# GraphSAGE mean aggregation on one core: 256 buckets' source features fetched by indirect row transfers, and two small kinds of ScalarE work moved to GpSimd

## The chip, the core and the metric

The kernel runs on one core of a Trainium2 chip. The metric is the device time of one execution in microseconds (us). Before the change it is 1871.68 us, the median of three runs (1863.13 to 1876.03).

The engines are named as in the profile: PE is TensorE, DVE VectorE, ACT ScalarE, POOL GpSimd, SP SyncE. SP issues DMAs from its own queue, POOL from another; each engine works through its instructions in the order in which they were written.

## The reference

800,000 edges join 12,500 nodes with 64 features each. For every edge the features of its source node are added to its destination node, the sums are scaled by `deg_inv`, and two 64 x 64 weight matrices are applied:

```python
N, deg, D = 12500, 64, 64
E = N * deg
nsum = _segment_sum(x[src], dst, N)
h_neigh = nsum * deg_inv[:, None]
return x @ w_self + h_neigh @ w_neigh
```

## The kernel before

**Sorting.** Each edge becomes one 32-bit key, made of the destination's block (77 blocks of 164 nodes), the source's block (98 blocks of 128 nodes), the destination's half block, the source's place in its block and the destination's place in its half. The pair of a destination block and a source block is a bucket; there are 77 * 98 = 7546, and a bucket has 128 slots (64 for each half of the destination block). The keys are sorted in 128 runs on DVE (`sort_runs`), cut into rows, gathered with indirect DMAs (`gather_runs` L533, `split_rows` L543) and merged (`merge_runs` L572). The rows come in three parts, with 29, 20 and 10 buckets to a row and 128 rows each: buckets 0 to 3711, 3712 to 6271, and the rest.

**Decoding a part** (L746 to L855). For each of a row's buckets, `find_and_gather` counts the keys below the bucket's first key (DVE, L708), turns the count into a position `ix` with one small ACT instruction (L762), and fetches a window `v` of keys around that position with an indirect DMA on POOL (L742). `decode_buckets` splits the window: the sources' places in their block go as a bfloat16 list `l` to the DRAM table `sl` (L794), one row of 128 slots per bucket, and the destinations' places are transposed by PE into the SBUF table `dlT`. Part 0 is decoded before the last stage begins; parts 1 and 2 are decoded inside it, between the steps described next. Keys that did not fit in a bucket's slots are found apart (`leftovers` L865); there are 127 groups of 128 of them.

**The last stage** (`nodes`, L943). Its loop walks the buckets in tiles of 8. `one_hots` (L924) prepares 28 buckets at a time: SP loads the 28 rows of `sl`, spread over all partitions, into `slb` (four DMAs, L933); DVE compares them with the partition's number and gets the one-hot matrices `ohs`, 128 sources by 128 slots for each bucket (L935); and it compares the destinations' places with a ramp and gets `ohd` (L940). `gather` then lets PE multiply each bucket's `ohs` with the source block's features `xh`, which stay in SBUF (L966; 128 fp16 numbers per node, 64 leading and 64 trailing parts). That puts the features of each slot's source into PSUM, `ct`; ACT copies the 8 buckets to SBUF as `xg` (L976), or DVE does, for some tiles of part 2 (L974). `sums` lets PE multiply `xg` with `ohd`, in two halves, into the accumulators `acc` (L1047). For the leftovers, POOL fetches 128 rows of features from the DRAM table `xt` with one indirect DMA into one of five buffers `lx` (L997), up to 616 buckets ahead, and PE adds them (L1015).

**What sets the order.** All these instructions are written in one order by hand: for each tile the loop writes a `gather`, every other tile two `sums`, in between a step of the part being decoded, and after that DVE merge steps for the next part, until `PACE` nanoseconds of them (420, later 405, by the program's own costs) are written per tile (L1361). So the merges ride along with the tiles, and DVE's queue holds both. SP's queue holds the loads of `slb`, each waiting for one of three buffers. POOL's queue holds the fetches of `lx`, `v` and `u` (the gathers of `split_rows`), and the writing of the outputs.

**Finishing** (L1105). When six destination blocks are done, PE multiplies the sums with the weights into `po`, ACT scales the result with `deg`, one instruction for each 123 nodes, as a copy from PSUM to SBUF (L1117), and in a later step POOL adds it to the output in DRAM (L1123).

Of the kernel before, what the change touches and what calls it, by code (L numbers as in the profile page):

```python
# [23 lines left out]
NB = 98  # L24
# [13 lines left out]
SPARE = TURN - BASE[2]  # L38
assert 128 * KPRS[2] < BASE[1]
# [4 lines left out]
        (32, 48, 72, 124, 204, 368, 676, 1264))  # L44
SUP = 8
# [6 lines left out]
PACE = (0, 420, 405)  # L52
# [20 lines left out]
LAG = 4  # L73
HELD = 5
OCT = 6
# [78 lines left out]
def constants():  # L154
# [15 lines left out]
    assert out["cx"].shape == (128, NCX)  # L170
    for p in range(NP):
# [202 lines left out]
class Kernel:  # L374
# [12 lines left out]
    def setup(self):  # L387
# [23 lines left out]
        self.cx = keep.tile([128, NCX], F32, name="cx")  # L411
        self.junkb = keep.tile([128, JUNKB], BF, name="junkb")
# [53 lines left out]
    def sort_edges(self, mps):  # L466
# [10 lines left out]
        with tc.tile_pool(name="raw", bufs=1) as raw:  # L477
            with tc.manual_schedule():
                self.make_keys(raw, a, mps)
                nc.sync.dma_start(self.c1, self.I["c1"])  # L480
                nc.sync.dma_start(self.cx, self.I["cx"])
                for p in range(NP):
                    nc.sync.dma_start(self.c2[p], self.I[f"c2_{p}"])
# [262 lines left out]
    def find_and_gather(self, part, vp):  # L746
# [8 lines left out]
        for k in range(kpr + LAG):  # L755
# [4 lines left out]
            if k >= LAG:  # L760
                g = k - LAG
                nc.scalar.activation(ix[:, g:g + 1], acc[:, g:g + 1], AF.Relu, bias=self.c2[part][:, 3, g:g + 1])  # L762
# [3 lines left out]
    def decode_buckets(self, part, v, vp, mps):  # L766
# [21 lines left out]
        def narrow(k, n, vk, w):  # L788
# [4 lines left out]
            rows = self.sl[BASE[part]:BASE[part] + 128 * kpr].rearrange("(r k) s -> r k s", k=kpr)  # L793
            (nc.gpsimd if part else nc.sync).dma_start(rows[:, k:k + n], l16[:, :n])  # L794
# [129 lines left out]
    def one_hots(self, pool):  # L924
# [3 lines left out]
        for c in range(0, NBID, 28):  # L928
            n = min(28, NBID - c)
# [4 lines left out]
            s = pool.tile([128, 28, 128], FH, name="ohs", bufs=3)[:, :n]  # L934
            nc.vector.tensor_scalar(s.rearrange("p c s -> p (c s)"), b, self.pidx[:, :1], None, op0=OP.is_equal)  # L935
            d = pool.tile([128, 14, HN, 2], FH, name="ohd", bufs=4)[:, :n // 2]
# [4 lines left out]
            yield [(s[:, j], d[:, j // 2, :, j % 2]) for j in range(n)]  # L941

    def nodes(self, pool, aps, mps):  # L943
# [3 lines left out]
        source = self.one_hots(pool)  # L947
        ready = []
        pend = []
        late = []  # L950
        done = []
        acc = None

        turn = 0

        def gather(b0, cnt, vector):
# [4 lines left out]
            while len(ready) < min(cnt + ahead, NBID - b0):  # L961
                ready.extend(next(source))
            cols = ready[:cnt]
            del ready[:cnt]
            for i in reversed(range(cnt)):
                nc.tensor.matmul(ct[:, i * 128:(i + 1) * 128], cols[i][0],  # L966
                                 self.xh[:, (b0 + i) % NB].rearrange("p a f -> p (a f)"), start=True, stop=True)
            xg = pool.tile([128, 1024], FH, name="xg", bufs=6)
            if vector and (len(ready) < min(8 + ahead, NBID - b0 - cnt) or NBID - b0 < 56):
# [3 lines left out]
            if vector and turn % 2:  # L973
                nc.vector.tensor_copy(xg[:, :cnt * 128], ct[:, :cnt * 128])  # L974
            else:
                nc.scalar.activation(xg[:, :cnt * 128], ct[:, :cnt * 128], AF.Copy)  # L976
            return b0, xg, [d for _, d in cols]
# [11 lines left out]
        def pick(b0):  # L989
            if self.picked == len(done) or len([u for u in uses if u[5]]) >= HELD:  # L990
# [11 lines left out]
        def spread(u):  # L1002
            o, p, c, f, e = u[:5]
            u[7] = pool.tile([128, 2, OCT * HN], FH, name="ohl", bufs=HELD)
            n = slice((f - o * OCT) * HN, (e - o * OCT) * HN)
            nc.vector.tensor_scalar(u[7][:, :, n], self.wide.rearrange("p (h n) -> p h n", h=2)[:, :, n],
# [4 lines left out]
        def add(u, stop=False):  # L1011
            o, _, _, f, e = u[:5]
            n = slice((f - o * OCT) * HN, (e - o * OCT) * HN)
            for h in range(2):
                nc.tensor.matmul(acc[h][:, n], u[5], u[7][:, h, n], start=False, stop=stop)  # L1015
# [11 lines left out]
        def sums(job):  # L1027
# [15 lines left out]
            for i, d in enumerate(cols):  # L1043
# [369 lines left out]
```

## Time and profile before

| | |
|---|---|
| median of three runs | 1871.68 us |
| the profiled execution | 1856.37 us |
| its span, first to last instruction | 1854.6 us |
| busy in the span: DVE, ACT, PE, POOL | 1718.2, 1116.7, 986.6, 576.2 us |
| first and last `ohs` matmul of the last stage (L966) | 804.6 and 1836.7 us |
| bytes read from HBM, written to it | 277.01, 26.52 MB |

The span's first 804.6 us are sorting, merging and decoding part 0, with DVE nearly alone at work; the last stage takes the rest. A group of instructions is shown as line, engine, operation, output<-input and shape, its count, busy time and mean duration in ns, and then the idle time of its engine just before it, with what ended that idle time. A window of the span is shown as from:to, its length, and then each engine's busy time with the number of its instructions in brackets; after that the granted TensorE clock, the share of the 16 DMA engines that was busy, and GB/s.

### The profile page before, as it was taken

The numbers are of one execution on the slowest core, as the hardware profiler recorded it, in microseconds if no ns is written. First come the engines' busy times: TensorE is split into PE (matmuls) and PEld (weight loads), VectorE is DVE, ScalarE is ACT, GpSimd is POOL, SyncE is SP. The second block draws the span as 40 slices with busy tenths as digits, with TensorE's granted clock in tenths as the row PEclk, the third lists the DMA queues.
The fourth block names the chain that finished last, engine by engine and source line by source line (L and its number), as shares of the span: only waits on it lengthen the run. The fifth ranks groups of instructions, "written<-read, shape, count | busy, mean of one in ns | idle before, by whom it ended". The sixth has DMA issues, their size and how long they took to land.

```text
span 1854.6 us, 54153 instructions
## 1 busy us (share of the span) xinstructions
PE 986.6 (53%) x23413; PEld 851.9 (46%) x23413; DVE 1718.2 (93%) x1718; ACT 1116.7 (60%) x1587; POOL 576.2 (31%) x447
## 2 busy tenths in 40 slices
PE   3046000000000000058979979897898899888996
PEld 1015000000000000057868868776887788777885
DVE  6999999999999999989989999998898799978885
ACT  5263000113001005458979989899999899977885
POOL 2000000055502005404456535473332523532331
PEclk7567555555555555579989999999999999999998
DMA  5207100021002002169978888996889788977894
GB/s 174 54 0 169 39 0 0 38 79 51 18 4 73 10 0 82 47 216 266 274 249 253 251 248 254 296 282 227 264 250 284 234 265 242 326 200 257 274 268 118
DMA packets 176789, 307.79 MB, mean 166 GB/s; under 512 B 127885, under 2 KB 133596, under 8 KB 175772
## 3 DMA queue, kind: packets, MB, share of 16 engines
q1 hardware_dynamic: 98268, 275.58, 44.9%
q0 software_dynamic: 78272, 28.65, 9.6%
q8 instruction: 185, 3.03, 0.7%
q14 instruction: 64, 0.52, 0.1%
HBM read 277.01 MB, written 26.52 MB: 164 GB/s over the span
## 4 chain that ended last, share of the span: by engine, by line
DVE 19%; PE 13%; DMA 11%; issue 10%; SPq 5%; POOL 4%; ACT 4%; DVEq 0%; POOLq 0%; ACTq 0%
DMA slb<-sl 10%; PE ct L966 7%; DVE u L328 7%; PE acc L1047 5%; SPq L933 5%; DVE ohs L935 4%; DVE ohd L940 3%; ACT xg L976 2%; DVE u L362 2%; POOL u L565 1%; POOL lx L997 1%; POOL out L1123 1%; DVE u L316 1%; DMA sl<-l 1%; PE acc L1015 1%
## 5 line engine op out<-in xcount | busy, mean ns | idle before, releaser
L976 ACT ACTIVATE xg<-ct 128x1024 f16<-128x1024 f32 x919 | 862.6, 1074 | 104.4 <-PE ct L966 80.0
L966 PE MATMUL ct<-xh,ohs 128*128 128x128 f16 x7546 | 532.6, 224 | 87.9 <-DVE ohs L935 23.7
L966 PEld LDWEIGHTS <-ohs 128*128 128x128 f16 x7546 | 451.8, 100 | 125.4 <-issue 52.5
L328 DVE TENSOR_TENSOR u<-u 128x1512 f32<-128x1512 f32 (+57 forms) x316 | 425.7, 1362 | 12.9 <-ACT u L312 8.6
L1047 PE MATMUL acc<-ohd,xg 64*128 64x82 f16 x15092 | 395.2, 201 | 47.7 <-ACT xg L976 20.4
L1047 PEld LDWEIGHTS <-xg 64*128 64x128 f16 x15092 | 324.6, 96 | 104.6 <-issue 29.2
L997 POOL DMA_INDIRECT lx<-xt,ls x127 | 232.0, 1826 | 425.6 <-PE acc L1015 352.5
L940 DVE TENSOR_TENSOR ohd<-iota,dlT 128x2296 f16<-128x2296 bf16 x270 | 362.2, 1341 | 0.0
L935 DVE TENSOR_SCALAR ohs<-slb,pidx 128x3584 f16<-128x3584 bf16 x270 | 321.8, 1192 | 40.2 <-DMA slb<-sl 19.0
L509 PE MATMUL stp<-cx,swapa 128*128 128x16 f32 (+1 forms) x12 | 3.1, 335 | 398.0 <-DVE swapa L505 398.0
L260 DVE TENSOR_TENSOR a<-b 128x1040 f32<-128x1040 f32 (+41 forms) x130 | 194.7, 1539 | 3.5 <-DVE b L260 0.5
L260 DVE TENSOR_TENSOR b<-a 128x1040 f32<-128x1040 f32 (+46 forms) x150 | 194.6, 1345 | 3.2 <-ACT a L262 0.4
L538 POOL DMA_INDIRECT u<-d,ixa x48 | 72.5, 1511 | 390.8 <-ACT junka L526 335.4
L509 PEld LDWEIGHTS stp<-cx,swapa 128*128 128x128 f32 x12 | 2.6, 271 | 398.5 <-DVE swapa L505 398.5
L312 ACT ACTIVATE u<-u 128x256 f32<-128x256 f32 (+14 forms) x60 | 33.0, 618 | 170.6 <-DVE u L316 134.8
L1123 POOL DMA_DIRECT2D out<-o x27 | 99.1, 3800 | 103.1 <-ACT o L1117 89.8
L802 PE MATMUL tr<-idb,l 128*128 128x128 bf16 x59 | 7.6, 263 | 188.9 <-ACT l L796 188.9
L262 ACT ACTIVATE b<-a 128x2 f32<-128x2 f32 (+31 forms) x41 | 15.9, 402 | 127.1 <-DVE a L260 120.4
L802 PEld LDWEIGHTS <-l 128*128 128x128 bf16 x59 | 4.3, 114 | 191.2 <-ACT l L796 190.8
L316 DVE TENSOR_TENSOR u<-u 128x2016 f32<-128x2016 f32 (+11 forms) x40 | 61.9, 1563 | 16.2 <-DMA u<-da,ixb 8.8
L262 ACT ACTIVATE a<-b 128x1 f32<-128x1 f32 (+24 forms) x34 | 8.6, 259 | 105.4 <-DVE b L260 99.9
L565 POOL DMA_INDIRECT u<-da,ixb x24 | 36.9, 1539 | 88.6 <-ACT ixb L513 85.0
(158 smaller groups left out, 839.4 us busy)
## 6 DMA issues: line engine op xcount, KB each, us to landing
slb<-sl SPq DMA_DIRECT2D x1076, 224.0 KB
xt<-xh SPq DMA_DIRECT2D x1, 3136.0 KB
out<-o POOLq DMA_DIRECT2D x25, 123.0 KB
own<-os SPq DMA_DIRECT2D x12, 256.0 KB
out<-os SPq DMA_DIRECT2D x12, 256.0 KB
rd<-dst SPq DMA_DIRECT2D x5, 512.0 KB
rs<-src SPq DMA_DIRECT2D x5, 512.0 KB
lx<-xt,ls POOLq DMA_INDIRECT x127
```

The lines of the kernel that those rows point to most:

```text
L260: nc.vector.tensor_tensor(view(dst, lo + sh, [[st, g], [1, l]]), x, y, op=op)
L316: nc.vector.tensor_tensor(at(oth, to, n), x, y, op=op)
L328: nc.vector.tensor_tensor(to, at(cur, ln + lo, n), at(cur, lo + k, n), op=op)
L538: nc.gpsimd.indirect_dma_start(out=u[:, i * w:(i + 1) * w], out_offset=None, in_=src, in_offset=bass.IndirectOffsetOnAxis(ap=self.start[pa ...
L933: nc.sync.dma_start(b[j::4], bass.AP(tensor=src.tensor, offset=src.offset, ap=[[0, 32], [1, n * 128]]))
L935: nc.vector.tensor_scalar(s.rearrange("p c s -> p (c s)"), b, self.pidx[:, :1], None, op0=OP.is_equal)
L940: nc.vector.tensor_tensor(d, self.iota[:, None].to_broadcast(wide), ix, op=OP.is_equal)
L966: nc.tensor.matmul(ct[:, i * 128:(i + 1) * 128], cols[i][0], self.xh[:, (b0 + i) % NB].rearrange("p a f -> p (a f)"), start=True, stop=True)
L976: nc.scalar.activation(xg[:, :cnt * 128], ct[:, :cnt * 128], AF.Copy)
L997: nc.gpsimd.indirect_dma_start(out=x, out_offset=None, in_=self.xt, in_offset=bass.IndirectOffsetOnAxis(ap=self.left[p][1][:, c:c + 1].bit ...
L1047: nc.tensor.matmul(acc[h][:, db % OCT * HN:(db % OCT + 1) * HN], xg[r, i * 128:(i + 1) * 128], d[r], start=db % OCT == 0 and sb == 0, stop ...
L1123: nc.gpsimd.dma_start(out, o[:n, at], accum_op=OP.add)
```

## The change

**Direct buckets.** In part 0 the bucket in column 15 of each row, in part 1 the one in column 11, is direct: 128 in each part, one in 29 and one in 20. A direct bucket has no row in `sl`, no `ohs`, no `L966` matmul and no place in `ct` and `xg`. Its list of sources is transposed by PE when its part is decoded (a tile `dt`), and three DVE instructions on 128 x 128 turn it into row numbers of `xt` (`dix`). In the last stage one indirect DMA on POOL per direct bucket fetches its 128 slots' rows from `xt` into one of 12 buffers `xd` (`bring`), at most one per tile, 160 buckets ahead of the tile; the `acc` matmul reads `xd` in place of a piece of `xg`. `ohd` is made as before, now by a generator of its own (`dest_hots`). A tile holds up to 8 buckets that are not direct, and the direct ones between them: there are 914 tiles in place of 950 (449, 305 and 160 by part, before 467, 322 and 161).

**Moved to POOL.** The position `ix` is made by a POOL `tensor_scalar` on 128 x 1 directly ahead of the fetch that reads it. In finishing, ACT copies `po` in one instruction for all 492 nodes, and POOL multiplies it in place with `deg` (123 x 256).

**Beside that**, `PACE` becomes 428 and 430, a leftover buffer is picked only when fewer than five are in use or were added in the last six tiles (`BACK`), and the leftovers' destination matrix `ohl` is stored narrower. The core of the diff:

```diff
+DCOL = (15, 11, None)
+KSRC = [k - (c is not None) for k, c in zip(KPRS, DCOL)]
+DIRECT = {BASE[p] + r * KPRS[p] + c: (p, r) for p, c in enumerate(DCOL) if c is not None for r in range(128)}
+NSRC = NBID - len(DIRECT)
+FETCH = 160
+FETCHED = 12
...
-PACE = (0, 420, 405)
+PACE = (0, 428, 430)
...
+DCH = 28
 HELD = 5
...
+BACK = 6
...
-                nc.scalar.activation(ix[:, g:g + 1], acc[:, g:g + 1], AF.Relu, bias=self.c2[part][:, 3, g:g + 1])
+                nc.gpsimd.tensor_scalar(ix[:, g:g + 1], acc[:, g:g + 1], self.c2[part][:, 3, g:g + 1], None, op0=OP.add)
                 self.gather_window(part, g, ix)
...
+            (nc.gpsimd if part else nc.sync).dma_start(rows[:, to:to + m], l16[:, :m])
+            if m < n:
+                ps = mps.tile([128, 128], BF, name="dt", tag="ct", bufs=3)
+                nc.tensor.transpose(ps, l16[:, m], self.idb)
+                u = vp.tile([128, 128], F32, name="du")
+                nc.vector.tensor_tensor(u, ps, self.dx[:, part], op=OP.add)
+                nc.vector.scalar_tensor_tensor(u, ps, 128.0, u, op0=OP.is_lt, op1=OP.mult)
+                self.direct[part] = self.keep.tile([128, 128], U32, name=f"dix{part}")
+                nc.vector.tensor_scalar(self.direct[part], u, float(N), None, op0=OP.add)
+                self.spent += 800
...
-        for c in range(0, NBID, 28):
-            n = min(28, NBID - c)
+        for c in range(0, NSRC, 28):
+            n = min(28, NSRC - c)
...
+        def bring(b0, most):
+
+            while most and coming and coming[0][0] <= b0 + FETCH and coming[0][1][0] in self.direct:
+                b, (p, r) = coming.pop()
+                coming.extend(islice(fetch, 1))
+                held[b] = pool.tile([128, 128], FH, name="xd", bufs=FETCHED)
+                nc.gpsimd.indirect_dma_start(
+                    out=held[b], out_offset=None, in_=self.xt,
+                    in_offset=bass.IndirectOffsetOnAxis(ap=self.direct[p][:, r:r + 1], axis=0))
+                most -= 1
...
+            own = [b for b in range(b0, b0 + cnt) if b not in DIRECT]
+            num = len(own)
...
+            parts = {b: xg[:, i * 128:(i + 1) * 128] for i, b in enumerate(own)}
+            return b0, [parts[b] if b in parts else held.pop(b) for b in range(b0, b0 + cnt)], dest
...
-            if self.picked == len(done) or len([u for u in uses if u[5]]) >= HELD:
+            busy = len([u for u in uses if u[5]]) + len([n for n in added if n > len(done) - BACK])
+            if self.picked == len(done) or busy >= HELD:
                 return
...
+        tiles = TILES
+        bring(0, 8)
         for t, (b0, cnt) in enumerate(tiles):
+            bring(b0, 1)
             pend.append(gather(b0, cnt, self.changed))
...
-            for b in range(b0, b0 + nb):
-                nc.scalar.activation(o[:n, b], po[:n, b], AF.Copy, scale=self.deg[:n, 4 * qq + b:4 * qq + b + 1])
+            at = slice(b0, b0 + nb)
+            nc.scalar.activation(o[:n, at], po[:n, at], AF.Copy)
+            scale = self.deg[:n, 4 * qq + b0:4 * qq + b0 + nb]
+            nc.gpsimd.tensor_tensor(o[:n, at], o[:n, at], scale[:, :, None].to_broadcast([n, nb, D]), op=OP.mult)
```

In the built program the lines of the changed kernel are other numbers: `xd` is fetched at L1016, `lx` at L1073, the multiplication with `deg` stands at L1196, the output's DMA at L1202, `ix` at L788 and the fetch of `v` at L768. Three places show how the instructions stand.

POOL in part 1, after the gathers of part 2's rows and up to the store of the merged rows. Before:

```order
L997 DMA lx<-xt,ls_16204 128x128 x3
L1123 DMA out<-o 123x4x64
L997 DMA lx<-xt,ls_16204 128x128
L1123 DMA out<-o 123x4x64
L997 DMA lx<-xt,ls_16204 128x128 x7
L1123 DMA out<-o 123x4x64
```

The same place in the changed kernel, as far as the second output (`dix_15020` holds part 1's row numbers):

```order
L1073 DMA lx<-xt,ls_16649 128x128
L1016 DMA xd<-xt,dix_15020 128x128 x3
L1196 TENSOR_TENSOR o<-o,deg 123x256
L1016 DMA xd<-xt,dix_15020 128x128 x2
L1073 DMA lx<-xt,ls_16649 128x128
L1202 DMA out<-o 123x4x64
L1016 DMA xd<-xt,dix_15020 128x128
L1073 DMA lx<-xt,ls_16649 128x128
L1016 DMA xd<-xt,dix_15020 128x128 x4
L1196 TENSOR_TENSOR o<-o,deg 123x256
L1073 DMA lx<-xt,ls_16649 128x128
L1016 DMA xd<-xt,dix_15020 128x128 x2
```

Between two fetches of `lx` now stand up to five of `xd`, and the multiplication stands some fetches ahead of the DMA that writes its result.

POOL where part 2's windows are fetched. Before:

```order
L595 DMA d_2_71<-u 128x1264
L742 DMA v<-d_2_71,ix_2_23618 128x200
L997 DMA lx<-xt,ls_16204 128x128
L742 DMA v<-d_2_71,ix_2_23618 128x200 x5
L997 DMA lx<-xt,ls_16204 128x128
```

In the changed kernel, the first of them:

```order
L621 DMA d_2_71<-u 128x1264
L1016 DMA xd<-xt,dix_15020 128x128 x2
L1073 DMA lx<-xt,ls_16649 128x128
L1016 DMA xd<-xt,dix_15020 128x128
L788 TENSOR_SCALAR ix_2_23846<-acc_2_23845,c_2_74 128x1
L768 DMA v<-d_2_71,ix_2_23846 128x200
L1016 DMA xd<-xt,dix_15020 128x128
L788 TENSOR_SCALAR ix_2_23846<-acc_2_23845,c_2_74 128x1
L768 DMA v<-d_2_71,ix_2_23846 128x200
L1016 DMA xd<-xt,dix_15020 128x128
```

Each fetch of `v` has its `ix` ahead of it on POOL itself, and fetches of `xd` between.

ACT around the finishing of six destination blocks in part 0. Before:

```order
L1054 ACTIVATE g<-acc_6437 128x6x82
L976 ACTIVATE xg<-ct 128x1024 x4
L1117 ACTIVATE o<-po,deg 123x64 x4
L976 ACTIVATE xg<-ct 128x1024 x15
L1117 ACTIVATE o<-po,deg 123x64 x4
```

In the changed kernel:

```order
L1132 ACTIVATE g<-acc_6467 128x6x82
L1050 ACTIVATE xg<-ct 128x1024 x2
L1194 ACTIVATE o<-po 123x256
L1050 ACTIVATE xg<-ct 128x1024 x15
L1194 ACTIVATE o<-po 123x256
```

Four small instructions became one.

More of the change, by code (lines that the diff above doesn't have):

```diff
@@ L951, in nodes @@
         done = []
+        added = []
         acc = None
         turn = 0
+        left = [NSRC, NBID]
+        fetch = iter(sorted(DIRECT.items()))
+        coming = [next(fetch)]
+        held = {}
+        def bring(b0, most):
[7 more added lines that the diff above has]
+                most -= 1
         def gather(b0, cnt, vector):
```

97 lines of the change are left out of this document (64 added, 33 removed).

## The prediction

> **What bounds the kernel now.** I first cut the span by stage (the view of busy time by window), at the first matmul of the last stage and at the points where the new fetches of part 0 and of part 1 end, 160 buckets ahead of the part's last one.
>
> ```profile
> 0.00:804.60 804.60, 75.01 (x274) 43.48 (x274) 762.27 (x575) 186.58 (x400) 153.04 (x206) 0.54 0.18 50
> 804.60:1301.00 496.40, 431.73 (x10837) 380.48 (x10838) 472.11 (x562) 452.78 (x577) 230.29 (x128) 0.96 0.86 262
> 1301.00:1650.00 349.00, 311.79 (x7867) 276.19 (x7867) 318.08 (x399) 326.77 (x433) 140.24 (x85) 0.97 0.85 259
> 1650.00:1854.60 204.60, 168.09 (x4447) 151.76 (x4441) 165.75 (x187) 150.57 (x180) 52.60 (x28) 0.95 0.76 229
> ```
>
> The columns after the length are PE, PEld, DVE, ACT, POOL. Until 804.6 the change has nothing to do. In the next two windows, which I call A and B, no engine alone is the bound: DVE is busy for 95% and 91%, ACT 91% and 94%, PE 87% and 89%, the DMA engines 86% and 85%. Only POOL has room: 46% and 40%. Next the view of waits, for 804.6 to 1650: who holds up PE, the end of the pipeline.
>
> ```profile
> POOL lx L997 <- PE acc L1015: 267.9, 57, 13.2
> POOL out L1123 <- ACT o L1117: 48.0, 11, 13.7
> PE ct L966 <- DVE ohs L935: 23.7, 19, 8.2
> PE ct L966 <- ACT xg L976: 20.8, 22, 3.8
> PE acc L1047 <- ACT xg L976: 20.4, 15, 4.8
> DVE ohs L935 <- DMA slb<-sl: 11.0, 12, 2.3
> ```
>
> PE loses 41 us to ACT and 24 to DVE. POOL's long waits are for a free `lx` buffer: POOL is early, and nobody waits for it.
>
> **What the change takes away.** The groups of instructions from 800 us on give the prices (busy time, mean ns, idle time before):
>
> ```profile
> L976 ACT ACTIVATE xg<-ct 128x1024 f16<-128x1024 f32 x906 | 857.8, 1080 | 103.7 <-PE ct L966 79.3 <-DMA slb<-sl 22.4 <-PE acc L1015 0.7
> L966 PE MATMUL ct<-xh,ohs 128*128 128x128 f16 x7546 | 532.6, 224 | 87.9 <-DVE ohs L935 23.7 <-ACT xg L976 22.3 <-DMA slb<-sl 22.0
> L935 DVE TENSOR_SCALAR ohs<-slb,pidx 128x3584 f16<-128x3584 bf16 x269 | 321.2, 1194 | 40.2 <-DMA slb<-sl 19.0 <-PE ct L966 18.9 <-PE acc L1047 1.0
> L1117 ACT ACTIVATE o<-po,deg 123x64 f32<-123x64 f32 x101 | 24.2, 351 | 7.5 <-PE po L1114 7.1
> L1054 ACT ACTIVATE g<-acc 128x492 f32<-128x492 f32 x22 | 12.4, 651 | 0.0
> L762 ACT ACTIVATE ix<-acc,c 128x1 uint32<-128x1 f32 x30 | 10.2, 339 | 0.0
> ```
>
> For part 0, so window A: DVE loses 128/28 = 4.6 `ohs`, 4.6 x 1.194 = 5.5 us (three instructions on 128 x 128 come back, about 1 us if each takes the 0.34 of ACT's smallest). ACT loses 18 tiles x 1.08 = 19.4, 20 `ix` x 0.339 = 6.8, and in 11 finishes four instructions of 0.351 for one on 123 x 256; that one lies between the 64 and the 492 columns above, 0.351 and 0.651, and I take 0.46, so 11 x (1.40 - 0.46) = 10.4. Together 37 of ACT's 453 us. PE loses 128 x 532.6/7546 = 9 us. `ohd`, `acc` and the merges stay. How much of this reaches the end? DVE holds the tightest queue in A, so its 4.5 net counts whole. Of PE's waits for ACT, A's share is 41 x 496/845 = 24 us; ACT falls from 91% to 84%, and I let a third of them go, 8: **A becomes about 13 us shorter**, between 5 (DVE alone) and 29 (all the waits go). The same sum for B gives 5.5 + 6, **11 us, if POOL lets it**. In the last window only seven finishes are touched: 0.
>
> **What the change adds to POOL.** First what one indirect fetch costs it. Two moments of the trace, POOL's timeline while DVE stands idle until 952.74, and while DVE works without a gap:
>
> ```profile
> 949.29 0.95 POOL L565 DMA_INDIRECT u<-da,ixb  x1 [0.16 <-issue]
> 951.86 0.94 POOL L997 DMA_INDIRECT lx<-xt,ls  x1 [0.30 <-issue]
> 952.74 1.69 DVE L316 TENSOR_TENSOR u<-u 128x1472 f32<-128x1472 f32 x1 [7.25 <-DMA u<-da,ixb]
> ...
> 1041.28 3.00 POOL L997 DMA_INDIRECT lx<-xt,ls  x1 [7.55 <-PE acc L1015]
> 1044.59 3.48 POOL L997 DMA_INDIRECT lx<-xt,ls  x1 [0.30 <-issue]
> ...
> 1041.73 1.37 DVE L328 TENSOR_TENSOR u<-u 128x1170 f32<-128x1170 f32 x1
> 1043.02 1.15 DVE L935 TENSOR_SCALAR ohs<-slb,pidx 128x3584 f16<-128x3584 bf16 x1
> 1044.08 1.35 DVE L940 TENSOR_TENSOR ohd<-iota,dlT 128x2296 f16<-128x2296 bf16 x1
> ```
>
> 0.95 us beside an idle DVE, 3.0 to 3.5 beside a busy one; and the first of these ends at 1044.28, 0.11 after DVE's `ohs` did (1044.17). So an indirect fetch waits for DVE's instructions to end, and 0.30 lies between two of them. The Trainium skill, SBUF — State Buffer, section Who interferes with whom, states it as a lock: GpSimd shares its SBUF port pair with DVE, and whichever comes second blocks fully; the trace agrees (0.95 against 3.48). That page's 3.1 us for such a DMA beside a DVE copy would make window B's 182 fetches 619 us long, far over its 349; the means below do not bear that out. The means, in A, in B, and in the densest stretch of POOL's work (1184 to 1250):
>
> ```profile
> L997 POOL DMA_INDIRECT lx<-xt,ls x70 | 138.7, 1981 | 178.0 <-PE acc L1015 130.3 <-DVE ls L905 37.1 <-issue 7.5
> L742 POOL DMA_INDIRECT v<-d,ix x20 | 28.7, 1434 | 21.9 <-ACT ix L762 19.8 <-issue 2.1
> L565 POOL DMA_INDIRECT u<-da,ixb x8 | 14.7, 1840 | 11.2 <-ACT ixb L513 9.9 <-issue 1.3
> ...
> L997 POOL DMA_INDIRECT lx<-xt,ls x36 | 61.7, 1713 | 141.4 <-PE acc L1015 137.6 <-issue 2.3 <-PE ct L966 1.2
> L742 POOL DMA_INDIRECT v<-d,ix x10 | 16.5, 1647 | 13.1 <-ACT xg L976 7.6 <-ACT ix L762 4.6 <-issue 0.9
> L565 POOL DMA_INDIRECT u<-da,ixb x8 | 11.1, 1387 | 1.5 <-issue 1.2 <-ACT ixb L513 0.3
> ...
> L742 POOL DMA_INDIRECT v<-d,ix x19 | 27.7, 1459 | 17.7 <-ACT ix L762 15.6 <-issue 2.1
> L997 POOL DMA_INDIRECT lx<-xt,ls x9 | 12.0, 1329 | 3.0 <-issue 1.5 <-PE acc L1015 0.9 <-PE ct L966 0.6
> ```
>
> With the 0.30 between, a fetch costs 1.25 at the least and 2.28 (A) or 2.01 (B) at the most. I take the dense stretch, since the new queue will be dense: (27.7 + 12.0)/28 + 0.30 = **1.72**. What is not an indirect fetch is 230.3 - 182.1 = 48 us in A and 140.2 - 89.3 = 51 in B. POOL's small arithmetic does not occur in the trace; between a tenth of a fetch and a whole one I take 0.8, half a fetch, for each `ix` and each product with `deg`. The Trainium skill's GPSIMD Engine Reference, section 3.1, has 4497 ns for such a product on 2048 numbers, by length 0.56 us for our 256 (an estimate); the sum would shrink by 5 in A and B together; no run here shows it.
>
> A: 128 + 98 = 226 fetches x 1.72 = 389, + 48, + 31 x 0.8 = 25: **462 of 496**, it fits. B: 128 + 54 = 182 x 1.72 = 313, + 51, + 19 x 0.8 = 15: **379 in 349**, 30 too many. What is queued behind a late fetch: on POOL everything, on PE the `acc` matmul that reads `xd`, and behind it all of PE, then ACT and DVE, whose buffers stay full. Cover is the lead of 160 buckets, at 349 us for part 1's 2560 buckets 22 us. Against it stands lateness brought along: from 1184 to 1250 POOL was idle for 20.7 us, and there it gets 16 `xd`, 19 `ix` and 2 products, 16 x 1.72 + 21 x 0.8 = 44, so 24 late, of which I let 10 be left at the start of B. PE then waits 30 + 10 - 22 = **18 us** in B, and B's own gain of 11 is void, since POOL sets the pace there. The products' wait for ACT (up to 13.7 above, as `out` has it now) stays below the lead.
>
> **The DMA engines.** In B their queues read:
>
> ```profile
> q1 hardware_dynamic: 17432, 83.27, 70.8%
> q0 software_dynamic: 27762, 6.03, 12.7%
> ```
>
> That is 0.227 and 0.0255 us of an engine per packet. 128 x 128 new rows take 418; 4.6 loads of `slb` less, at 17432/90 = 194 packets each, give back 203. The share goes from 85% to 89%. I cost it at nothing: `slb` has three buffers, and DVE waits 11 us for it now. Uncovered it would be those 11 again.
>
> **The sum.** On the profiled execution, 1856.4: -13 + 18 = +5. That execution lies 15 below the median, so the median goes from 1871.7 to **1877 us, no change** by the 1% (19 us) that a measurement of this kernel can tell. Its own range: 1862 to 1890.
>
> **The rivals.** *POOL keeps up.* At 1.5 a fetch (two thirds of the way down from B's mean with the gap to 1.25), B needs 182 x 1.5 + 66 = 339 of 349; no stall, and 13 + 11 = 24 us are won: 1848, with all the ACT waits gone 1835. For it: whenever POOL is late DVE soon idles, and a fetch beside an idle DVE is 0.95. Against: DVE must first have been stopped. *POOL becomes the bound in both windows.* From about 1.85 on A is full. At 1.9, A needs 226 x 1.9 + 73 = 502 and B 182 x 1.9 + 66 = 412; 6 + 63 + 10 - 22 = 57 us of stall, a third of it mended by the quicker fetches beside a stalled DVE: +38, 1910. For it: the 1.98 of A. Against: those were lone fetches, the dense ones were shorter. *DVE is held up by POOL's arithmetic.* The output's DMA shows how that looks:
>
> ```profile
> 1061.40 4.18 POOL L1123 DMA_DIRECT2D out<-o  x1
> 1062.08 2.24 DVE L935 TENSOR_SCALAR ohs<-slb,pidx 128x3584 f16<-128x3584 bf16 x1
> 1066.89 1.14 DVE L935 TENSOR_SCALAR ohs<-slb,pidx 128x3584 f16<-128x3584 bf16 x1
> ```
>
> An `ohs` beside it took 2.24 in place of 1.14. If each of the 27 products costs DVE as much, that is 27 x 1.1 = 30 on top of the sum: 1907. Against: a product is a quarter as long as that DMA. *The transfers.* `slb` comes late by 11 to 20 us: 1892.
>
> **How the numbers follow.** No change 0.37, POOL keeps up 0.31, POOL the bound 0.22, DVE held up 0.06, transfers 0.04. Faster by over 1%: 0.31; within: 0.37; slower: 0.32. The range runs from the second case's 1838 to the third's 1914.
>
> **What would show it.** In the profile after: `xd` fetches at a mean near 1.4 us; POOL busy above 90% in B and hardly waiting for `lx` buffers; `acc` matmuls waiting for the DMA into `xd`, some 18 us in B and none in A; ACT near 85% in A. It is wrong if PE never waits for `xd`, if it does so in A, or if `ohs` is stretched beside the products.

## The result, and the profile after

The change makes the kernel slower by a tenth: 2058.99 us, the median of 4 runs (2044.29 to 2062.42), against 1873.86 (1863.13 to 1882.86); ratio 1.0995, 95% interval 1.0951 to 1.1039. The prediction said 1877, 1838 to 1914. Later the same, unaltered kernel took 1985.09 on another chip, beside 1862.29 for the kernel before there: 1.0654 (1.0577 to 1.0731). So there are two losses to explain, one that came both times and one that did not. The kernel before was profiled on the first occasion only; its medians on the other chips, 1858.74 to 1865.45, lie within 0.9% of the first, so I hold all windows against that one profile.

First the execution that was profiled for the result, 2060.75 us. Busy time by window, bounded at the same buckets as in the prediction, but from the first `acc` matmul on and up to the last. A and B before (the last window there is 180.1 us):

```profile
808.30:1305.20 496.90, 431.43 (x10890) 380.23 (x10890) 472.90 (x571) 454.43 (x580) 230.29 (x128) 0.96 0.86 261
1305.20:1658.40 353.20, 313.27 (x7865) 277.58 (x7861) 322.28 (x404) 326.22 (x431) 140.24 (x85) 0.96 0.85 258
```

All three after:

```profile
811.50:1406.30 594.80, 478.94 (x10775) 407.72 (x10776) 476.59 (x547) 438.93 (x514) 420.92 (x280) 0.86 0.74 218
1406.30:1843.60 437.30, 342.33 (x7731) 288.80 (x7725) 316.62 (x388) 309.17 (x374) 336.52 (x227) 0.86 0.69 207
1843.60:2042.10 198.50, 170.16 (x4352) 153.40 (x4346) 163.09 (x200) 144.17 (x157) 53.36 (x37) 0.94 0.78 229
```

A is 98 us longer, B 84, the last window 18. DVE and ACT do about the work of before (476.6 and 438.9 us in A; 472.9 and 454.4), spread over more time, and POOL, which the prediction watched, is busy for 71% of A and 77% of B. So something makes all of them wait. Three of PE's waits from 804 us on (total, times, longest):

```profile
PE acc L1125 <- issue: 114.6, 181, 2.3
PE ct L1040 <- issue: 40.0, 86, 1.6
...
PE acc L1125 <- DMA xd<-xt,dix: 9.6, 5, 7.1
```

The wait that I had forecast, for `xd`, is there with 9.6 us. The long one is "issue": idle time that ended with no visible event, 155 us in 267 pieces, where the kernel before has 23.3 (11.4, 10.1 and 1.8). What it looks like is in the timeline (most of the matmuls beside these weight loads are left out):

```profile
1459.42 0.35 PEld L1040 LDWEIGHTS <-ohs 128*128 128x128 f16 x4 [1.29 <-issue]
1460.07 0.95 POOL L1073 DMA_INDIRECT lx<-xt,ls  x1 [0.30 <-issue]
1460.15 0.10 PEld L1040 LDWEIGHTS <-ohs 128*128 128x128 f16 x1 [0.39 <-issue]
1460.86 0.31 PEld L1040 LDWEIGHTS <-ohs 128*128 128x128 f16 x3 [0.61 <-issue]
1461.33 0.95 POOL L1016 DMA_INDIRECT xd<-xt,dix  x1 [0.30 <-issue]
1461.57 0.27 PE L1040 MATMUL ct<-xh,ohs 128*128 128x128 f16 x1 [0.25 <-issue]
1462.27 0.13 PEld L1040 LDWEIGHTS <-ohs 128*128 128x128 f16 x2 [1.11 <-issue]
```

PE runs a few instructions every 0.70 to 0.73 us (1459.42, 1460.15, 1460.86, 1461.57, 1462.27) and stands still between, and the profile shows nothing that it waits for. The longest such stretches last some 16 us (1547 to 1563); two of 12 and 10 follow each other from 1263 to 1287. POOL meanwhile issues fetches back to back at 0.95 + 0.30 us, since DVE, behind PE, hardly works either (2.95 of the 14 us from 1452 on). I call this starving; the name says what it looks like, not what causes it.

Then the same kernel on the other chip (label r1_change_again), with the same bounds; after them PE's waits there, and the two longest of B alone:

```profile
811.50:1373.70 562.20, 441.67 (x10777) 391.93 (x10778) 473.36 (x548) 436.12 (x513) 472.77 (x281) 0.89 0.78 231
1373.70:1772.10 398.40, 310.62 (x7727) 277.44 (x7722) 310.48 (x387) 306.52 (x374) 330.91 (x225) 0.88 0.77 227
1772.10:1971.00 198.90, 169.15 (x4353) 153.07 (x4349) 161.80 (x199) 145.05 (x157) 56.94 (x38) 0.93 0.77 227
```

```profile
PE acc L1125 <- DMA xd<-xt,dix: 82.6, 24, 11.0
PE ct L1040 <- DVE ohs L975: 57.9, 19, 21.3
PE acc L1125 <- ACT xg L1050: 45.4, 12, 19.7
...
PE acc L1125 <- issue: 8.3, 10, 2.6
...
PE acc L1125 <- DMA xd<-xt,dix: 27.3, 6, 7.9
PE acc L1125 <- ACT xg L1050: 27.0, 6, 19.7
```

Here nothing starves. A is 65 us longer than before, B 45, the last window 19, and PE waits 82.6 us for `xd`: 55.3 in A, 27.3 in B. In A PE's idle time grew by 55 us (562.2 - 441.7 against 496.9 - 431.4), in B by 48. B's second long wait comes from POOL too: ACT stands still for 20.2 us up to 1742.95, because the store of `sl` whose buffer it needs is queued on POOL behind `ix`, `v`, `xd` and `lx`, and PE waits 19.7 us of that for `xg`. This is the picture that the prediction had described, POOL too late, but far larger. The remaining 10 us of A are PE's own: 441.7 us busy against 431.4 for fewer matmuls, at a granted clock of 0.89 against 0.96. Whether that adds to the loss or only follows from PE's idling is not shown. POOL's fetches in A, then in B:

```profile
L1016 POOL DMA_INDIRECT xd<-xt,dix x122 | 224.9, 1843 | 35.8 <-issue 34.3 <-PE ct L1040 0.6 <-PE acc L1125 0.3
L1073 POOL DMA_INDIRECT lx<-xt,ls x70 | 131.3, 1875 | 33.5 <-issue 13.1 <-DVE ls L945 12.8 <-PE ct L1040 5.5
...
L768 POOL DMA_INDIRECT v<-d,ix x20 | 25.1, 1255 | 5.6 <-POOL ix L788 5.6
L788 POOL TENSOR_SCALAR ix<-acc,c 128x1 uint32<-128x1 f32 x20 | 19.5, 974 | 0.6
...
L591 POOL DMA_INDIRECT u<-da,ixb x8 | 9.6, 1206 | 4.1 <-DMA da<-u 2.7 <-issue 1.4
```

```profile
L1016 POOL DMA_INDIRECT xd<-xt,dix x126 | 194.7, 1545 | 40.5 <-issue 21.5 <-PE ct L1040 9.4 <-PE acc L1125 7.1
L1073 POOL DMA_INDIRECT lx<-xt,ls x36 | 51.8, 1438 | 10.8 <-issue 6.6 <-PE ct L1040 1.8 <-DMA out<-o 0.8
```

In A the 220 fetches take 390.9 us, 1.78 each, and with 0.30 between them 2.08; the prediction had 1.72. POOL's busy 472.8 and 220 x 0.30 = 66 are 539 of A's 562 us; in B 331 + 180 x 0.30 = 54 are 385 of 398. POOL is full in both windows, but for 4% of A and 3% of B.

### The profile page after: what moved, and what is told of

It is laid out like the page before. It is cut to its first block, busy times and chain, and to the rows that moved or that the text cites. A ratio compares the mean times of both kernels' runs of the same rounds, so it can differ in the third digit from the quotient of the medians.

```text
span 2059.0 us, 53837 instructions
## 1 busy us (share of the span) xinstructions
PE 1079.8 (52%) x23159; PEld 905.3 (44%) x23159; DVE 1723.5 (84%) x1713; ACT 1082.3 (53%) x1448; POOL 975.3 (47%) x760
## 5 line engine op out<-in xcount | busy, mean ns | idle before, releaser
L1050 ACT ACTIVATE xg<-ct 128x1024 f16<-128x1024 f32 x885 | 840.4, 1041 | 308.5 <-remote 132.7
L1040 PE MATMUL ct<-xh,ohs 128*128 128x128 f16 x7290 | 561.6, 232 | 81.7 <-issue 40.0
L1040 PEld LDWEIGHTS <-ohs 128*128 128x128 f16 x7290 | 467.0, 104 | 131.3 <-issue 100.7
L1125 PE MATMUL acc<-ohd,xg 64*128 64x82 f16 x14580 | 443.1, 207 | 150.4 <-issue 112.2
L1125 PEld LDWEIGHTS <-xg 64*128 64x128 f16 x14580 | 350.5, 99 | 229.7 <-issue 159.3
L1016 POOL DMA_INDIRECT xd<-xt,dix x256 | 393.2, 1536 | 119.1 <-issue 63.1
L975 DVE TENSOR_SCALAR ohs<-slb,pidx 128x3584 f16<-128x3584 bf16 (+1 forms) x261 | 318.1, 1219 | 110.4 <-remote 45.7
L1073 POOL DMA_INDIRECT lx<-xt,ls x127 | 199.2, 1568 | 154.6 <-PE acc L1093 88.2
L1202 POOL DMA_DIRECT2D out<-o x27 | 100.2, 3724 | 0.9 <-POOL o L1196 0.8
L1196 POOL TENSOR_TENSOR o<-o,deg 123x256 f32<-123x256 f32 (+2 forms) x27 | 31.7, 1233 | 143.1 <-ACT o L1194 142.9
```

The lines of the kernel that those rows point to most:

```text
L975: nc.vector.tensor_scalar(s, b, self.pidx[:, :1], None, op0=OP.is_equal)
L1016: nc.gpsimd.indirect_dma_start(out=held[b], out_offset=None, in_=self.xt, in_offset=bass.IndirectOffsetOnAxis(ap=self.direct[p][:, r:r + 1 ...
L1040: nc.tensor.matmul(ct[:, i * 128:(i + 1) * 128], cols[i], self.xh[:, own[i] % NB].rearrange("p a f -> p (a f)"), start=True, stop=True)
L1050: nc.scalar.activation(xg[:, :num * 128], ct[:, :num * 128], AF.Copy)
L1073: nc.gpsimd.indirect_dma_start(out=x, out_offset=None, in_=self.xt, in_offset=bass.IndirectOffsetOnAxis(ap=self.left[p][1][:, c:c + 1].bit ...
L1125: nc.tensor.matmul(acc[h][:, db % OCT * HN:(db % OCT + 1) * HN], x[r], d[r], start=db % OCT == 0 and sb == 0, stop=False)
```

## The experiments

Kernels measured together ran on one chip, each beside the kernel before there; all ratios are to that.

**What makes PE starve** (first chip). The change without the moves; all but the fetches; the fetches without readers; the same tiles filled by plain transfers from SP's queue:

```diff
 e1_fetches_only: ix and o as before, on ScalarE
 e2_moves_only
-DCOL = (15, 11, None)
+DCOL = (None, None, None)
 e3_unread: as e2_moves_only, dix and the 256 fetches kept
+FCOL = (15, 11, None)
-        fetch = iter(sorted(DIRECT.items()))
+        fetch = iter(sorted(COMING.items()))
 e4_plain_sp
-                nc.gpsimd.indirect_dma_start(out=held[b], ...)
+                nc.sync.dma_start(held[b], self.xt[b % NB * 128:b % NB * 128 + 128])
```

> The 256 row transfers stay, the gather positions and the output scaling go back to ScalarE's small operations. Theory A (the row transfers that POOL issues make PE's own instructions come late: PE idles with nothing to wait for): 2040 to 2080 us, the weight loads' idle time put to issue stays near 262 us. Theory B (POOL's new small arithmetic beside the fetches is to blame): at most 1900 us, that idle time back near the 82 us of the kernel before.

> No bucket is fetched directly (all source features by one-hots, as before); positions and scaling on POOL as in the change, and so are the split one-hot generators and the smaller spread tiles. Theory A: PE's idle time put to issue falls back to some 80 us in its weight loads, and the time is that of the kernel before or a little under it, 1840 to 1880 us (ScalarE gives up some 17 us of small work in the last stage's first two windows). Theory B: near 2050 us.

> All buckets go by one-hots again, and the 256 row transfers are issued at the same places all the same, into tiles that nothing reads; no part of the result is left out. Theory A (issuing is enough): PE starves as in the change, 2030 to 2120 us (up to 18 us more one-hot work than the change), idle time put to issue 200 us or more. Theory C (it is the reading side: products that take their weights from many small transferred tiles, each with its own wait): 1850 to 1900 us, idle time put to issue near 82 us. What POOL itself takes for 256 more fetches is in both.

> The 256 tiles are filled by plain transfers of 128 consecutive rows from the sync queue, not by indirect ones from POOL (so the sums of these buckets get other rows than they should); the reading side is as in the change. Theory A: no starving, 1830 to 1880 us, idle time put to issue near 82 us. Theory C: near 2050 us. Theory D (the packets of 256 bytes on the DMA engines, whoever issues them, hold up the instructions): also near 2050 us, and then e3 is slow too, which C denies.

Measured: 1.1016 (1.0952 to 1.1080), 1.0126 (1.0076 to 1.0176), 1.0910 (1.0836 to 1.0985), 1.0158 (1.0111 to 1.0206). The idle time of the weight loads put to issue, their two largest rows, of the unread fetches and of the plain transfers:

```profile
PEld L1126 <- issue: 156.6, 278, 2.0
PEld L1041 <- issue: 92.7, 149, 22.5
```

```profile
PEld L1038 <- issue: 47.4, 85, 3.0
...
PEld L1123 <- issue: 37.8, 77, 3.6
```

249 against 85 us; the kernel before has 82. So on this chip PE starves when POOL issues the 256 indirect fetches, even if nothing reads them, and not when SP brings as many rows into the same tiles: theory A holds here, and B (POOL's arithmetic), C (the readers) and D (the small packets) fall. Whether it takes an indirect fetch, or any transfer that POOL issues, was not tested on this chip. In e2_moves_only the loss of 1.3% was a surprise; theory A had expected no loss.

**Rows, number, kind** (second chip). Plain transfers from POOL; 64 rows a fetch; every other fetch (both unread):

```diff
 e5_plain_pool
-                nc.gpsimd.indirect_dma_start(out=held[b], ...)
+                nc.gpsimd.dma_start(held[b], self.xt[b % NB * 128:b % NB * 128 + 128])
 e6_half_rows, on e3_unread
-                    in_offset=bass.IndirectOffsetOnAxis(ap=self.direct[p][:, r:r + 1], axis=0))
+                    in_offset=bass.IndirectOffsetOnAxis(ap=self.direct[p][:64, r:r + 1], axis=0))
 e8_every_other, on e3_unread: COMING only with
+ r in range(0, 128, 2)
```

> As the run with plain transfers of 128 consecutive rows, but POOL issues them (the sums of these buckets get other rows than they should). If any transfer that POOL's own queue carries makes PE starve: 2000 us or more, idle time of the weight loads put to issue above 200 us. If only the indirect ones do: 1870 to 1920 us, beside the 1897 of the same transfers from the sync queue, idle time put to issue near 85 us.

> The 256 fetches that nothing reads, each with 64 rows in place of 128; nothing of the result is left out. The fetches cost 2040 - 1887 = 153 us with 128 rows. If the loss goes by rows (what POOL writes for each row): half of it, 1964 us (1930 to 2000). If it goes by the number of indirect instructions: 2040 us (2010 to 2070).

> 128 of the 256 fetches that nothing reads, every other one, with 128 rows each; nothing of the result is left out. If each fetch costs PE the same: half of the 153 us, 1964 us (1930 to 2000). If PE starves only where fetches follow each other closely: well under half, 1890 to 1925 us.

Measured: 1.0119 (1.0082 to 1.0156), 1.0561 (1.0532 to 1.0591), 1.0258 (1.0226 to 1.0289). Each time fell where one theory had it, and I first read this as starving that goes by rows and sets in sharply. The traces say otherwise: the weight loads' issue idle is 75, 72 and 68 us. None of the three starves, and the 64-row fetches lose their 102 us (1963.31 against 1861.11) in another way. Their group on POOL, and DVE's three longest single waits there:

```profile
L1017 POOL DMA_INDIRECT xd<-xt,dix x253 | 404.5, 1599 | 74.1 <-issue 71.1 <-DMA xd<-xt,dix 1.2 <-DMA lx<-xt,ls 0.9
```

```profile
DVE du L831 <- PE dt L829: 32.0, 1, 32.0
DVE u L340 <- DMA u<-da,ixb: 27.5, 2, 17.9
DVE w L809 <- DMA v<-d,ix: 18.3, 1, 18.3
```

With half the rows a fetch holds POOL as long as with all (1.60 us, and as much in the same run for the 127 fetches of `lx`, which kept their 128 rows), and what stands behind the fetches in POOL's queue, the gathers of `u` and `v` and the stores of `sl`, comes late and stops DVE. With plain transfers, a mean of 0.93 us, POOL keeps up:

```profile
812.20:1317.80 505.60, 425.72 (x10773) 377.69 (x10774) 470.84 (x547) 434.82 (x513) 340.26 (x274) 0.93 0.85 255
1317.80:1673.80 356.00, 304.36 (x7731) 269.45 (x7725) 312.68 (x389) 307.53 (x374) 242.76 (x227) 0.94 0.84 254
```

```profile
L1016 POOL DMA_DIRECT2D xd<-xt x250 | 191.9, 929 | 44.9 <-PE acc L1123 30.5 <-DMA out<-o 9.7 <-DMA xd<-xt 3.0
```

A and B are then 9 and 3 us longer than before, not 65 and 45.

**Paced fetches, half the bytes, stores moved** (third chip). A memset of 128x256 behind each unread fetch; unread fetches with 128 rows of half the width; the change with its stores of `sl` on SP:

```diff
 e11_paced, on e3_unread
+                nc.gpsimd.memset(self.space, 0.0)
 e12_half_bytes, on e3_unread
-                    out=held[b], out_offset=None, in_=self.xt,
+                    out=held[b][:, :64], out_offset=None, in_=self.xt.rearrange("n (a f) -> (n a) f", a=2),
 e13_change_store_sp
-            (nc.gpsimd if part else nc.sync).dma_start(rows[:, to:to + m], l16[:, :m])
+            nc.sync.dma_start(rows[:, to:to + m], l16[:, :m])
```

> The 256 fetches of 128 rows that nothing reads, each followed on POOL by a memset of 128x256, so that no two fetches follow each other within 1.25 us; nothing of the result is left out. If PE starves by the rate of rows (above some 100 rows per us): the weight loads' idle time put to issue falls from 249 to under 120 us although the rows and the instructions are the same, and the time to 1900 to 2010 us (POOL later by 256 x 0.7 us or more). If it goes by the number of rows: 200 us of that idle time or more, 2040 us or more.

> The 256 fetches that nothing reads, each with 128 rows of 64 numbers in place of 128 numbers (half the bytes, as many rows; the rows are others, which nothing reads; nothing of the result is left out). If it goes by rows: PE starves as with whole rows, 2000 to 2060 us, idle time put to issue above 180 us. If it goes by bytes: as with 64 rows, 1940 to 1985 us, idle time near 72 us.

> The change with the stores of the source lists of part 1 on the sync queue. VectorE's single stop of 24 us for the list of fetches of part 1 (it waits for PE's transpose, that for ScalarE, that for a store queued behind POOL's fetches) should shrink to a few us; PE's starving stays. If stops and starving add up: 2035 us (2020 to 2050). If the stop only overlaps with the starving: 2050 to 2065 us.

Measured: 1.0658 (1.0634 to 1.0681), 1.0566 (1.0542 to 1.0589), 1.0616 (1.0596 to 1.0636). The first two fell once more where a rate of rows, or of bytes, had them, with 81 and 73 us of issue idle. The last overthrew that reading: the expectation had the starving stay, and it was gone (60 us), although PE, DVE, ACT and POOL have the change's instructions in the change's order nearly to the end of A, where the change had lost 98 us and this kernel 61. So either where things lie in memory decided, or the chip did.

**The change again, beside three relatives** (fourth chip). Unaltered; with the feature table elsewhere in HBM; with 12 small loads more at the start; with the stores on SP once more:

```diff
 e14_memory_shift
-        self.sl = self.dram.tile([NCOL, 128], BF, name="sl")
+        self.sl = self.dram.tile([NCOL + 3000, 128], BF, name="sl")
 e15_more_loads
+                for i in range(12):
+                    nc.sync.dma_start(self.dx[:1, 0, i * 8:i * 8 + 8], self.I["dx"][:1, i * 8:i * 8 + 8])
```

> The change itself, unaltered, beside three relatives on one chip. So far all kernels that starve (the change, it without the moves, the unread fetches) ran on other occasions than those that do not. If starving belongs to the program: 1.0995 again, idle time of the weight loads put to issue above 240 us. If it belongs to the occasion (the chip, what else it does): near the 1.062 of the change with the stores on the sync queue, idle time below 100 us.

> The change with the source list's table in HBM 3000 rows longer than it is used, so that the feature table behind it lies elsewhere; every engine's instructions are the same, in the same order with the same waits. If starving comes from how tables and instructions lie in HBM: below 1.07 while the change itself stays at 1.0995. If not: as the change itself on this chip.

> The change with 12 loads of 32 bytes more on the sync queue in the first stage, long before PE's last stage; they only shift which semaphores and instruction addresses are used. If starving comes from such placement: below 1.07 while the change itself stays at 1.0995. If not: as the change itself on this chip.

> The change with the stores of part 1 and 2 on the sync queue, again, now beside the change itself. If the stores made the difference: 1.062 again, with the change at 1.0995. If the occasion did: both alike, but for the 24 us of VectorE's stop.

Measured: 1.0654 (1.0577 to 1.0731), 1.0659 (1.0591 to 1.0726), 1.0703 (1.0635 to 1.0772), 1.0605 (1.0547 to 1.0663). All alike, none starves (56 us of issue idle in the unaltered change): the occasion decides, the chip or what else went on, and which of these stays open. It also voids what I had drawn on the starving from comparing e6_half_rows, e8_every_other, e11_paced and e12_half_bytes with e3_unread, and e5_plain_pool with e4_plain_sp: they ran on other chips.

The stores show how POOL's lateness reaches the other engines. In the unaltered change here, from the waits of DVE and those of ACT in A:

```profile
DVE du L830 <- PE dt L828: 23.2, 1, 23.2
```

```profile
ACT l L836 <- DMA sl<-l: 14.7, 1, 14.7
```

ACT waits for a buffer whose store stands on POOL behind `xd`, `ix` and `v`, PE's transpose for the list of fetches waits for ACT, and DVE, ahead of its next `ohd` and `ohs`, for PE. With the stores on SP both waits are gone, and so is ACT's stop of 20.2 us in B; yet the ratio hardly moves (1.0605), and PE still waits 76.6 us for `xd`. DVE then waits 48.0 us in place of 16.2 for `slb`, whose loads share SP's queue with the stores. That is not the reason that the ratio stays: when the same kernel ran on the third chip, DVE waited 19.6 us for `slb`, and the ratio was 1.0616. POOL stays full there too: 463.1 us and 219 x 0.30 = 66 are 529 of the 548 us from 812.9 to 1361.

**Direct buckets in part 0 alone** (fifth chip; moves undone):

```diff
 e17_part0_only, on e1_fetches_only
-DCOL = (15, 11, None)
+DCOL = (15, None, None)
```

> Direct buckets in part 0 alone, 128 in place of 256, and the moves undone. With the fetch price of the unaltered change (1.68 + 0.30 us) POOL needs 226 x 1.98 + 48 = 495 us in the first window, as long as the window, and has room in the second. If POOL's lateness is what costs: PE waits at most 25 us for the tiles, and the time is 0.995 to 1.020 of the kernel before. If every fetch costs something whatever POOL's load: half of the change's loss, 1.030 or more. If PE starves on this occasion: its weight loads' idle time put to issue is above 150 us, and the time 1.04 or more.

Measured: 1.0243 (1.0200 to 1.0285), above the 1.020 that lateness had been given. Its two windows, and PE's wait for `xd`, all in A:

```profile
811.70:1348.50 536.80, 434.52 (x10776) 386.27 (x10777) 469.18 (x546) 441.48 (x564) 450.85 (x250) 0.90 0.80 241
1348.50:1707.00 358.50, 313.83 (x7850) 277.76 (x7845) 322.65 (x427) 322.40 (x426) 150.75 (x86) 0.95 0.83 254
```

```profile
PE acc L1125 <- DMA xd<-xt,dix: 40.1, 10, 10.4
```

A loses 40 us, with POOL full again (451 + 66 = 517 of 537) even without the moved arithmetic; B, where POOL has room, loses 5. The loss sits where POOL is full, and is about PE's wait for `xd` there. That A lost 65 us in the whole change is not settled by this: the list of part 1, absent here, stops DVE for 23.2 us there, but with the stores on SP and without that stop A was still 61 us longer.

**The moves by themselves** (second, third and fifth chip). Both moves on the kernel before; the same with the stores on SP; the scaling alone, its product placed ahead of the output's transfer:

```diff
 e9_before_moves
-                nc.scalar.activation(ix[:, g:g + 1], acc[:, g:g + 1], AF.Relu, bias=self.c2[part][:, 3, g:g + 1])
+                nc.gpsimd.tensor_scalar(ix[:, g:g + 1], acc[:, g:g + 1], self.c2[part][:, 3, g:g + 1], None, op0=OP.add)
-                nc.scalar.activation(o[:n, b], po[:n, b], AF.Copy, scale=self.deg[:n, 4 * qq + b:4 * qq + b + 1])
+            nc.scalar.activation(o[:n, at], po[:n, at], AF.Copy)
+            nc.gpsimd.tensor_tensor(o[:n, at], o[:n, at], scale[:, :, None].to_broadcast([n, nb, D]), op=OP.mult)
 e10_store_sp: as e9_before_moves, with the store of e13_change_store_sp
 e16_scaling_late: ix stays on ScalarE, tensor_tensor behind the yield
```

> The kernel before with nothing changed but the gather positions and the output scaling, which go to POOL. By the prediction's step (ScalarE gives up 17 us in window A, 10 in B, and PE's waits for it shrink by a third): 1850 to 1860 us. If that relief is void: within 0.5% of the kernel before. If POOL's products hold up DVE as its long transfers do: 1885 us or more. The run with all of the change but the fetches stood 1.3% above the kernel before; if that came from the moves, this stands there too, if from the order of the one-hots and the other new spacings, it does not.

> The kernel before with the two moves to POOL (1.0090 of the kernel before), and with the stores of the source lists of parts 1 and 2 on the sync queue in place of POOL's. If the moves lose their 16 us because POOL, late with the positions, stores late and ScalarE waits for the buffer (16.1 us, once): that wait is gone and the ratio is at most 1.000, down to 0.993 if ScalarE's relief then counts. If they lose it elsewhere: 1.006 to 1.012 as before.

> The kernel before with the output scaling alone on POOL, and its product placed directly ahead of the output's transfer, 40 buckets later than in the change; the gather positions stay on ScalarE. If both moves lost 0.9% because the positions' arithmetic waits on POOL for VectorE (1.21 us each, beside 0.28 us of waiting) and made POOL late, not because of the product: 0.993 to 1.001 of the kernel before. If the product itself does harm: 1.005 or more.

Measured: 1.0090 (1.0056 to 1.0124), 1.0108 (1.0084 to 1.0132), 1.0053 (1.0030 to 1.0076). ACT's relief never shows. In the first, one wait of ACT stands out, 1.4 us in the kernel before:

```profile
ACT l L791 <- DMA sl<-l: 16.1, 1, 16.1
```

A store behind `ix` and `v` on POOL comes late: in the stretch ahead of it, 1184 to 1270 us, an `ix` takes POOL 1.49 us and the `v` behind it waits another 0.27; ACT took 0.34. With the stores on SP that wait is gone, and DVE waits for `slb` instead:

```profile
DVE ohs L935 <- DMA slb<-sl: 46.6, 20, 7.0
```

It was 16.7 with the stores on POOL. Moving the wait gained nothing, so that run can't settle what the 16 us were worth. The scaling alone is still slower by half a per cent; why, I can't show. No kernel tried beats the kernel before.

## Why the prediction was wrong

**The step that failed, where nothing starves, is POOL's price in A**: 1.72 us a fetch, taken from the densest stretch of before "since the new queue will be dense", so that A came to 462 of 496 us and "fits". Measured is 2.08 in A (1.79 in B). With these the sum's own formula gives 226 x 2.08 + 73 = 543 us for a window of 497, and 182 x 1.79 + 66 = 392 for 353.

Density was not what made the fetches of that stretch short. Lone fetches of before, up to 1184 us, then the dense ones of the change up to 1230, both while DVE merges:

```profile
L997 POOL DMA_INDIRECT lx<-xt,ls x56 | 119.0, 2124 | 173.3 <-PE acc L1015 129.4 <-DVE ls L905 37.1 <-issue 4.6
...
L1016 POOL DMA_INDIRECT xd<-xt,dix x94 | 184.7, 1964 | 27.3 <-issue 26.1 <-PE ct L1040 0.6 <-PE acc L1125 0.3
L1073 POOL DMA_INDIRECT lx<-xt,ls x56 | 114.0, 2035 | 29.3 <-DVE ls L945 12.8 <-issue 9.2 <-PE ct L1040 5.2
```

A dense fetch cost nearly what a lone one had (1.96 and 2.04 us against 2.12), with the gap 2.26 to 2.34, about the upper bound of 2.28 that I had kept for the range. With every other fetch left out (e8_every_other, up to 1240 us) the mean is 1.95 too. What did differ is DVE's work: 396 instructions in 365.2 us up to 1184, so 0.92 each, and 90 in 63.2, so 0.70, in the stretch from 1184 to 1250, where keys are counted; in the change up to 1230 it is 0.92 again. That fits the prediction's own reading, that a fetch waits for DVE's instructions to end, but no run varied their length.

POOL is the bound in both windows, the second rival. I gave it 1910 because I stopped at 1.9 a fetch and let a third of the stall be mended by quicker fetches beside a stalled DVE. Such fetches exist (0.94 to 1.02 us from 1319 to 1339, while DVE stands still), and A's mean with them is still 1.78; A lost 65 us, more than the formula's 46, and B 45, more than its 39. The price alone therefore does not give the whole loss; the rest belongs to what follows.

**Who waits** was half right. `acc` waits for `xd`, but 55.3 us in A, where I had none, and 27.3 in B, where I had 18. Left out were the others in POOL's queue: `u` (DVE waits 25.1 us), `v` (14.4) and the store of `sl` (PE waits 19.7 us behind it in B). "What is queued behind a late fetch: on POOL everything" stood in the text; priced was only `xd`.

**The new list of fetches.** I took its three DVE instructions for about 1 us. For part 1 they stop DVE once for 23.2 us, and for 23.9 in the first execution (only 7.6 with the positions on ScalarE), because they stand in DVE's queue ahead of `ohd` and `ohs` and wait for PE, ACT and a store.

**The gains.** 13 us in A came nowhere to light. Where POOL keeps up (plain transfers), A is 505.6 against 496.9; it holds one stop of 18.5 for the list, without which it would be some 10 shorter than before. That the gain is hidden in there is an argument, not shown. The moves by themselves lose 0.9%.

**Two sums of the text do not come out.** With all of ACT's waits gone its terms (29 us in A, 5.5 + 17 in B) give about 1820, not 1835. And the ends of the range, 1838 and 1914, are not the values worked out for the two rivals, 1848 and 1910.

**Right were** POOL's other work (73 us in A; measured 473 - 391 = 82, of it 35.6 for `ix` and the products where I had 25) and the DMA engines (their share falls to 78%, `slb` stays at 16.2 us of waiting). That POOL's products would cost DVE little was right as well, though `ohs` is stretched beside them: in the second execution the 13 `ohs` that overlap a product by more than 0.2 us take 1.47 us in the mean, those that touch none 1.18, together some 4 us.

The last window is 18 and 19 us longer in the two executions. In the second 11 us of that is PE's idle time and 8 its longer busy time (granted clock 0.93 against 0.99). Of the idle time 6.9 us are lateness of POOL once more: DVE waits 8.9 us for `many`, a transfer that POOL issues, and PE for the `ohs` behind it. In the first that wait is 0.7 us; what lengthens the window there stays open. Of the signs that I had named, `xd` comes at a mean of 1.68 us where I had 1.4, POOL is full in B with the gaps counted (97%) and in A too, and ACT is at 78% in A, not 85%, since A grew. Two of the three signs of being wrong came: PE waits for `xd` in A, and `ohs` is stretched beside the products.

**No step had the starving.** The first execution is longer by a further 74 us (2059 - 1985), 33 in A and 39 in B; 12 us lie between the kernel before on the two occasions as well (1873.86 and 1862.29). The feedback in it, PE stops, DVE stops, fetches come at 0.95 us and PE stops again, fits the timeline but was not tested: the runs that should have tested it were on chips where nothing starves.

## What to carry to other kernels

Take the price of an instruction that waits for a neighbour from the stretch where the neighbour does the work that it will be doing, not from the one that is as crowded, and fill the window with it; when it comes to more than the window, price every other thing in that queue, not only the new ones. Before reading a cause out of two kernels that were measured on different chips, measure one of them again beside the other.

## What the runs showed of the hardware that was not expected

An indirect fetch holds POOL nearly by the instruction, not by rows or bytes: 1.60 us with 64 rows and 1.65 with rows of half the width, where the whole fetches of `lx` in the same runs take 1.60 and 1.62. The shortest ones are 0.90 us with 64 rows and 0.94 with 128. A plain transfer of the same tile from POOL's queue holds it 0.93 in the mean, where `lx` takes 1.78.

In the first execution and on the chip of the first experiments PE ran in small pieces, some 0.72 us apart, while POOL issued indirect fetches densely, and with no wait that the profile shows. The granted clock reads 0.50 in such a stretch (1452 to 1466 us), but so it does from 200 to 300 us in the kernel before, where PE has nothing to do, so it does not tell cause from effect. The queue that brings instructions shows nothing of it; its row after, before it was 185 packets:

```profile
q8 instruction: 183, 3.00, 0.6%
```

A packet took 1.04 us in the mean, 1.05 before. The Trainium skill, Runtime: NRT & Kernel Launch, section Instruction fetch mechanics, says that an engine's instructions are refilled in blocks of 16 KiB while the current ones run, at a cost that is mostly hidden. The packets agree (16384 bytes each). In number and mean time they are as before, so nothing in this row explains the stretches; what holds PE there no run shows.
